# Hashed attention and a SwiGLU block: who adds up the sums for the last block, and when two rows are rounded

## The chip, the core and the metric

The kernel runs on one core of a Trainium2 chip, as one program. The metric is the device time of an execution in microseconds. Five engines work side by side, each through its own instructions: TensorE (PE in the profile; its weight loads are PEld), VectorE (DVE), ScalarE (ACT), GpSimd (POOL) and SyncE (SP), which here only issues DMAs. Transfers are issued from SP, ACT and POOL.

## The reference

Attention in which a query sees only keys of its own hash bucket, and then a gated feed-forward block on its output, cut to what matters:

```python
# q, k, v: (4, 8, 768, 64) float32; proj: (64, 6)
q_bucket = sum over bits of (q @ proj > 0) * 2**bit        # k_bucket likewise
scores = where(q_bucket == k_bucket, q @ k.T / 8, -1e9)
attn = exp(scores - max) / sum
x = (attn @ v), heads side by side                         # (3072, 512)
g, val = x @ w_gate, x @ w_val                             # (512, 1536), float64
out = (g * sigmoid(g) * val) @ w_out                       # w_out (1536, 512), float64
```

The change touches only the second half, the feed-forward block.

## The kernel before, in words

**Blocks.** The 3072 tokens are worked on in three blocks of 1024 (`NB` = 3). Attention ends at about 314 us of the profiled execution. In the first two blocks there are twelve rows of the hidden layer, f = 0 to 11, of 128 features each. A row has an *up product* U f: four pieces (`atoms_of`), the first products `a` of gate and of value, then the second products `n` of gate and of value. Every operand is split into a rounded high part, a low part and their scaled difference, so that TensorE's products keep the precision: `a` is the product of high and low, `n` the correction. ScalarE copies `a` into the bank of `n` (L852), the second product is added onto it, ScalarE makes the gate from it (L865), VectorE the product of gate and value (L876). The result is rounded into `hid` in a *tail*: high part on ScalarE (L885), low part and difference on VectorE (L896, L899). A tail runs a given number of pieces later, counted in `tails`.

**Down products.** After three rows each stands a *down product* D n: eight chunks of 128 tokens. From the second part on, a chunk's accumulator is first copied into PSUM (`sow`, L927); after the product ScalarE copies the sum back (L972) and VectorE subtracts the correction (L978). So the order in the second block is U0 to U3, D0, U4 to U6, D1, U7 to U9, D2, U10, U11, D3. PSUM is four pairs of banks taken in turn: chunk 4 of a down product takes the pair of chunk 0 and can begin when chunk 0's L972 and L978 are done.

**The third block** computes its up products with fewer multiplications: over pairs of rows, in the manner of Strassen and Winograd, with seven products in place of eight. It needs sums of weight pieces and four sums of x. These are made *during the second block*, in tiles `made` (tag x2 for gate and for the first of x's sums, x3 for value and for the second), rounded there as well, and stored in DRAM (`sums_ram`, `xsums`) until the third block loads them. For each of six pairs of rows (p = 0 to 5) and for gate and value: `keep_w` adds the parts of the even row (VectorE, L1089), `add` the odd row and then the four combinations (L1102 to L1111), then come `high` (ScalarE, L1131), `low` and `diff` (VectorE, L1137 and L1156 for weights, L1139 and L1159 for x). `low` and `diff` each issue a store from SP. A tile x2 or x3 can be written again only when its stores have landed.

**Which engine adds.** In `add` before, gate's weight sums run on VectorE, value's on GpSimd for p = 0 to 4 and on VectorE for p = 5 (which is made at the end of the first block). All of x's sums, xa, xb, ya, yb, run on GpSimd (L1119 to L1125): two subtractions for the first of a pair, four for the second.

**The order around the change** is written by hand. `at_` and the loop over xa, xb, ya, yb name, for each sum, after which piece its steps are recorded: "U 5 3" is after piece 3 of row 5, "D 1 4" after chunk 4 of down product 1. What is recorded earlier stands earlier on its engine. The loads of weights from DRAM into the six ring buffers (`bring`, L308) are issued from POOL, in the same order as its sums; the stores and the loads of x are issued from SP.

Of the kernel before, what the change touches and what calls it, by code (L numbers as in the profile page):

```python
# [13 lines left out]
ALU = mybir.AluOpType  # L14
# [5 lines left out]
def kernel(  # L20
# [31 lines left out]
    nc = tc.nc  # L52
    PSUM = bass.MemoryType.PSUM
    B, H, S, D = q.shape
# [6 lines left out]
    NP = H // 2  # L61
# [3 lines left out]
    NF = DF // P  # L65
    PIECE = 512
# [70 lines left out]
    n = 0  # L137
# [654 lines left out]
    def gated_block(scope):  # L792
# [11 lines left out]
        LAST = NB - 1  # L804
# [248 lines left out]
        tails = []  # L1053
# [10 lines left out]
        def split_x(block, pr):  # L1064
            return split(raw_x.pop((block, pr)), block, pr, 0, WB)

        raw_x = {}
# [6 lines left out]
        made = {}  # L1074
        kept_w = {}
        tt = nc.vector.tensor_tensor
        k0, k1 = slice(0, HP), slice(HP, PIECE)

        def make(key, load=True):

            kind, n, side = key
            t = made[key] = xparts_p.tile([P, 2, 3, PIECE], FP32, tag=f"x{2 + side}", name="made")
            if load:
                for e in range(2):
                    nc.sync.dma_start(t[:, e, 0::2], ram[place["gv"[side], 2 * n + e]].bitcast(FP32)[:, 0:2])
# [3 lines left out]
            tt(w, held[what, F][:, 0].bitcast(FP32), held[what, F][:, 1].bitcast(FP32), op=ALU.add)  # L1089

        def add(key, F=None):

            kind, n, side = key
            tt = (nc.vector if kind == "w" and (F is None or side == 0) else nc.gpsimd).tensor_tensor
            if kind == "w":
                if F is not None:
                    make(key, False)
                t = made[key]
                if F is not None:
                    piece = held["gv"[side], F].bitcast(FP32)  # L1100
                    a, c = kept_w.pop("gv"[side]), t[:, 1, 2]
                    tt(c, piece[:, 0], piece[:, 1], op=ALU.add)  # L1102
                else:
                    a, c = t[:, 0, 2], t[:, 1, 2]
                    tt(a, t[:, 0, 0], a, op=ALU.add)
                    tt(c, t[:, 1, 0], c, op=ALU.add)
                s1, s2, s3, s4 = t[:, 0, 1, k0], t[:, 0, 1, k1], t[:, 1, 1, k0], t[:, 1, 1, k1]
                tt(s1, c[:, k0], c[:, k1], op=ALU.add)
                tt(s3, a[:, k0], c[:, k0], op=ALU.subtract)
                tt(s2, s1, a[:, k0], op=ALU.subtract)  # L1110
                tt(s4, a[:, k1], s2, op=ALU.subtract)  # L1111
                return
            make(key, False)
            t = made[key]
            b11, b12, b21, b22 = (raw_x[LAST, n + e][:, half * PIECE : (half + 1) * PIECE]
                                  for e in (0, NP // 2) for half in range(2))
            one, two_ = t[:, 0, 1], t[:, 1, 1]
            if side == 0:
                tt(one, b12, b11, op=ALU.subtract)  # L1119
                tt(two_, b22, one, op=ALU.subtract)  # L1120
            else:
                tt(one, b22, b12, op=ALU.subtract)
                tt(two_, b12, b11, op=ALU.subtract)
                tt(two_, b22, two_, op=ALU.subtract)
                tt(two_, b21, two_, op=ALU.subtract)  # L1125
                for e in (0, NP // 2):
                    raw_x.pop((LAST, n + e))

        def high(key):
            t = made[key]  # L1130
            nc.scalar.activation(r32(t[:, :, 0]), t[:, :, 1], AF.Copy,  # L1131
                                 scale=TOWARD if key[0] == "w" else TOWARD / STEP)
# [30 lines left out]
        def add_late(key, F):  # L1163
            add(key, F)
            bring()
# [8 lines left out]
        def put(kind, f, at, op, *args):  # L1174
            plan.setdefault((kind, f, at), []).append(lambda: op(*args))
# [7 lines left out]
        put("U", 0, 3, low, first_v)  # L1183
        put("U", 0, 3, diff, first_v)
        at_ = {
            0: ("U 1 1", "U 1 3", "U 2 1", "U 2 2", "U 2 3", "U 2 3", "U 3 0", "U 3 0"),
            1: ("U 3 1", "U 3 3", "D 0 2", "D 0 3", "D 0 4", "D 0 4", "D 0 5", "D 0 6"),
            2: ("U 5 3", "U 6 0", "U 6 1", "U 6 2", "U 6 3", "D 1 0", "D 1 1", "D 1 2"),
            3: ("U 7 3", "U 8 0", "U 8 1", "U 8 2", "U 8 3", "U 8 3", "U 9 0", "U 9 1"),
            4: ("U 9 3", "D 2 0", "D 2 2", "D 2 3", "D 2 4", "D 2 5", "D 2 6", "D 2 7"),  # L1190
        }

        def spot(text):
            kind, f, at = text.split()
            return kind, int(f), int(at)

        for p in range(NG - 1):
            g, v = ("w", p, 0), ("w", p, 1)
            F = (LAST - 1) * NF + 2 * p
# [12 lines left out]

        put("U", 4, 1, bring, NQ - 1)
        xa, xb, ya, yb = (("x", j, side) for j in range(2) for side in range(2))
        for key, here in ((xa, ("D 0 6", "U 4 2", "U 4 3", "U 4 3")), (xb, ("U 4 0", "U 5 0", "U 5 1", "U 5 1")),
                          (ya, ("D 1 3", "D 1 6", "D 1 7", "U 7 0")), (yb, ("D 1 4", "U 7 1", "U 7 2", "U 7 2"))):
            for text, op in zip(here, (add, high, low, diff)):
                put(*spot(text), op, key)

        xs = {}  # L1220
# [44 lines left out]
        for i, (kind, n) in enumerate(order):  # L1265
            b, f = divmod(n, NF if kind == "U" else NF // NQ)
            if b == LAST - 1:
                if kind == "U" and f == NF - 2:
                    assert not made
                    steps = first_quarter()  # L1270
                    put("U", f, 2, steps[0])
                    put("U", f, 3, steps[1])
                    put("U", f + 1, 0, steps[2])
                    put("U", f + 1, 0, load_x, LAST, (NP - 1,))
                    put("U", f + 1, 1, bring_sum, 0, xparts_p, "x3")
            elif (kind, f) == ("D", NF // NQ - 2):
                load_x(b + 1, range(NP // 2))
            elif kind == "U" and f >= NF - 2:
                assert len(added) == NPIECE
                splits.extend(split_x(b + 1, f - NF + 2))  # L1280
                if f == NF - 1:
                    load_x(b + 1, range(NP // 2, NP))
            for at, atom in enumerate(gens.pop(i, None) or atoms_of(kind, n)):
                if kind == "U" and at == 2:
                    sow_next(i)
                tail = atom()
                for entry in list(tails):
                    entry[0] -= 1
                    if not entry[0]:
                        tails.remove(entry)  # L1290
                        entry[1]()
                if tail:
                    tails.append([1 if n % NF == NF - 1 else 2, tail])
                if kind == "U" and f >= NF - 2 and at and splits:
                    splits.pop(0)()
                if kind == "D" and f == NF // NQ - 1:
                    if at == 0:
                        more = [split_x(b + 1, pr) for pr in range(NP // 2, NP)]
                        if b == LAST - 1:
                            for i_ in (1, 2):  # L1300
                                bring_sum(i_, xparts_p, f"x{i_ - 1}")
                    if b == LAST - 1:
                        if at in (1, 2, 5, 7, 8, 9):
                            more[at in (2, 7, 9)].pop(0)()
                        if at in (0, 5, 7):
                            fourth_sum()
                    elif at in (0, 7, 10):
                        for x in more:
                            x.pop(0)()
                count[0] += 1  # L1310
                if left and count[0] in (4, 6, 11):
                    left.append(left.pop(0)())
                    left[:] = [f for f in left if f]
                    if count[0] == 4:
                        bring(2)
                if kind == "U":
                    pace = (1, 2, 2, 2)
                elif n == 0:
                    pace = (0, 0, 0, 2, 1, 2, 2, 2)
                else:  # L1320
                    pace = (0, 0, 1, 0) + (1,) * 8
                if b == LAST - 1:
                    for op in plan.pop((kind, f, at), ()):
                        op()
                    continue
                if b == LAST - 2 and (kind, f) == ("D", NF // NQ - 1):
                    for op, key in opening.get(at, ()):
                        op(key)
                for _ in range(pace[at]):
                    step = next(mine, None)  # L1330
                    if step:
                        step()
# [173 lines left out]
    with ExitStack() as scope:  # L1506
        gated_block(scope)
# [32 lines left out]
```

## Time and profile before

| what | value |
|---|---|
| three runs | 903.12, 909.99 and 901.87 us, median 903.12 |
| profiled execution | 907.07 us, of which the span from first to last instruction is 905.2 |
| mean granted TensorE clock | 0.998 |
| second block in the profile | 511 to 721 us |
| second block (515 to 717 us), busy us | PE 192.13, PEld 155.58, DVE 137.05, ACT 93.98, POOL 68.84 |
| the same, DMA engines | 0.83 busy, 309 GB/s |
| L1102 to L1111 on VectorE | 5 instructions, 0.68 us for 512 columns, 0.42 for 256 |
| L1102 to L1111 on GpSimd | 1.3 to 2.4 us for 512 columns, 0.74 to 1.8 for 256 |
| L1119 to L1125 on GpSimd | 1.3 to 2.2 us each |
| ring load, from issue to landing | 6.9 us (median), 768 KB |

How to read the lines: L852 is line 852 of the kernel; `n<-a` is what is written and what is read, by the program's names; `x8` is how many instructions stand in one line of a timeline; the bracket gives the idle time of that engine before it and what ended it. Times are microseconds from the start of the span.

### The profile page before, as it was taken

Reading aid. Unit: us, or ns where it says so; the run is one execution under the profiler, and the core shown is the slowest. Engines: PE = TensorE matmul, PEld = TensorE weight load, DVE = VectorE, ACT = ScalarE, POOL = GpSimd, SP = SyncE. Lnnn points to the kernel's source line nnn. Section 1 sums busy time; section 2 is a strip of 40 time slices with the busy share of each in tenths; the row PEclk is TensorE's granted clock in tenths of the full one; section 3 lists DMA queues with packets and bytes.
Section 4 is the critical chain, followed back from the end, with each engine's and each line's share of the span. In section 5 each row is a group of like instructions: output and inputs, shape, how many; then the busy total and the mean of one; then the engine's idle time right before and its main releaser. Section 6 shows DMA issues by size and latency. Waiting matters only on the chain.

```text
span 905.2 us, 12871 instructions
## 1 busy us (share of the span) xinstructions
PE 891.1 (98%) x4731; PEld 624.6 (69%) x4731; DVE 671.2 (74%) x840; ACT 532.0 (59%) x782; POOL 158.5 (18%) x248
## 2 busy tenths in 40 slices
PE   9999999999999999999999999988999999999998
PEld 5444444444444488888888788866878788888887
DVE  6779999989999956649484968658673768377387
ACT  6788988788888645541424244344363677276460
POOL 2001100010101210101010021525342122121120
PEclk9999999999999999999999999999999999999999
DMA  7657788878988699776757777686879998397382
GB/s 181 110 146 181 188 209 189 204 184 249 223 190 228 220 356 351 268 266 215 277 193 275 290 305 279 239 330 244 325 289 388 381 341 332 113 339 274 147 289 93
DMA packets 155934, 224.08 MB, mean 248 GB/s; under 512 B 104320, under 2 KB 114016, under 8 KB 155488
## 3 DMA queue, kind: packets, MB, share of 16 engines
q0 software_dynamic: 25312, 128.99, 40.4%
q1 hardware_dynamic: 128576, 90.98, 34.5%
q10 hardware_dynamic: 1984, 3.29, 1.1%
q8 instruction: 37, 0.61, 0.3%
q14 instruction: 25, 0.20, 0.1%
HBM read 157.81 MB, written 64.59 MB: 246 GB/s over the span
## 4 chain that ended last, share of the span: by engine, by line
PE 87%; DVE 4%; DMA 3%; issue 3%; POOL 2%; ACT 1%; SPq 0%; POOLq 0%; DVEq 0%; ACTq 0%
PE o L809 19%; PE sc L605 17%; PE a L809 16%; PE av L636 14%; PE n L809 8%; PE y L809 6%; DMA xsums<-made 2%; PE x L809 2%; PE joint L677 1%; PE z L809 1%; PE joint L497 1%; DMA ring<-ram 1%; DVE o L978 1%; DVE o L974 1%; PE idle L431 0%
## 5 line engine op out<-in xcount | busy, mean ns | idle before, releaser
L809 PE MATMUL o<-ring,hid 128*128 128x512 f32 (+1 forms) x872 | 200.9, 389 | 4.0 <-ACT o L927 3.6
L809 PEld LDWEIGHTS o<-ring,hid 128*128 128x128 f32 x872 | 162.1, 188 | 41.2 <-ACT o L927 5.2
L809 PE MATMUL a<-xparts,ring 128*128 128x512 f32 x768 | 179.6, 392 | 2.6 <-DMA ring<-ram 2.6
L809 PEld LDWEIGHTS a<-xparts,ring 128*128 128x128 f32 x768 | 145.0, 189 | 33.9 <-issue 3.6
L615 ACT ACTIVATE A<-sc 128x768 f32<-128x768 f32 x192 | 154.0, 815 | 1.6 <-PE sc L605 0.8
L605 PE MATMUL sc<-qT,kT 64*128 64x384 f32 x768 | 153.0, 483 | 0.0
L852 ACT ACTIVATE n<-a 128x1024 f32<-128x1024 f32 x46 | 46.3, 1008 | 142.8 <-PE a L809 139.4
L636 PE MATMUL av<-A,vraw 128*64 128x386 f32 (+1 forms) x768 | 127.7, 488 | 0.0
L308 POOL DMA_DIRECT2D ring<-ram x108 | 61.1, 567 | 299.7 <-PE n L809 105.4
L636 PEld LDWEIGHTS av<-A,vraw 128*64 128x64 f32 x768 | 53.7, 136 | 73.3 <-issue 62.4
L605 PEld LDWEIGHTS sc<-qT,kT 64*128 64x128 f32 x768 | 68.8, 187 | 39.9 <-issue 35.3
L809 PE MATMUL n<-xparts,ring 128*128 128x512 f32 x384 | 91.7, 390 | 3.6 <-ACT n L852 3.6
L978 DVE TENSOR_TENSOR o<-o 128x512 f32<-128x512 f32 x84 | 56.9, 685 | 43.4 <-ACT o L972 28.0
L809 PEld LDWEIGHTS n<-xparts,ring 128*128 128x128 f32 x384 | 71.8, 188 | 19.7 <-ACT n L852 4.9
L896 DVE SCALAR_TENSOR_TENSOR hid<-hid,v 128x1024 fp32r<-128x1024 f32 (+1 forms) x26 | 29.8, 1145 | 69.4 <-ACT hid L885 69.4
L605 PE MATMUL sc<-qb,kb 64*128 64x384 bf16 x384 | 63.5, 323 | 0.0
L972 ACT ACTIVATE o<-o 128x512 f32<-128x512 f32 x56 | 33.0, 596 | 46.1 <-PE o L809 45.4
L659 DVE SCALAR_TENSOR_TENSOR both<-A 128x1536 f32<-128x1536 f32 x32 | 55.5, 1733 | 3.9 <-ACT A L615 2.5
L663 DVE TENSOR_TENSOR both<-both,A 128x1536 f32<-128x1536 f32 x32 | 55.9, 1748 | 1.7
L809 PE MATMUL y<-xparts,ring 128*128 128x512 f32 x216 | 54.8, 389 | 0.0
L203 POOL DMA_DIRECT2D ram<-stage x22 | 12.0, 546 | 204.8 <-DVE stage L201 96.1
L809 PEld LDWEIGHTS y<-xparts,ring 128*128 128x128 f32 x216 | 40.5, 188 | 8.4
(224 smaller groups left out, 1123.0 us busy)
## 6 DMA issues: line engine op xcount, KB each, us to landing
ring<-ram POOLq DMA_DIRECT2D x96, 768.0 KB, 6.9
ring<-sums_ram POOLq DMA_DIRECT2D x24, 768.0 KB, 6.6
ram<-stage POOLq DMA_DIRECT2D x22, 768.0 KB, 5.3
sums_ram<-made SPq DMA_DIRECT2D x12, 1024.0 KB
ram<-stage SPq DMA_DIRECT2D x14, 768.0 KB
vraw<-in_v_dram SPq DMA_DIRECT2D x16, 384.0 KB
words<-xram SPq DMA_DIRECT2D x12, 512.0 KB
sums_ram<-made SPq DMA_DIRECT2D x12, 512.0 KB
```

The source lines that it names most:

```text
L203: queues[0].dma_start(ram[i].bitcast(FP32), st)
L308: nc.gpsimd.dma_start(t.bitcast(FP32)[:, :, cols], src[:, :, cols])
L605: nc.tensor.matmul(banks_of[u][:, h], x["k", n][rows, ks], x["q", n][rows, qs], start=start, stop=stop)
L615: nc.scalar.activation(weights(u)[:, :, 0:HQ], banks_of.pop(u), AF.Exp, scale=SCALE * (1.0 if units[u][0] else OFF / 2))
L636: nc.tensor.matmul(ps[h * D : (h + 1) * D, 0:width], raws["v", n][:, h, c, :], a[:, h, 0:width], start=c == 0, stop=c == NCH - 1)
L659: nc.vector.scalar_tensor_tensor(out=t, in0=first, scalar=S * EPS / P / 2, in1=now, op0=ALU.add, op1=ALU.add)
L663: nc.vector.tensor_tensor(t, t, now, op=ALU.add)
L809: nc.tensor.matmul(ps, w, x, start=start, stop=stop, **more)
L852: nc.scalar.activation(n_, a, AF.Copy, scale=-(STEP + 1))
L896: nc.vector.scalar_tensor_tensor(out=l_, in0=h_.bitcast(FP32), scalar=-STEP, in1=v_, op0=ALU.mult, op1=ALU.add)
L972: nc.scalar.activation(accs[c], t[:, 0], AF.Copy, scale=STEP + 1)
L978: nc.vector.tensor_tensor(accs[c], accs[c], t[:, 1], op=ALU.subtract)
```

## The change

In the second block all weight sums are made on VectorE. Of x's sums GpSimd makes the first subtraction of each of the four (`open_x`), VectorE the others, some pieces later. Steps are recorded at other pieces: value's `add` of p = 2, 3 and 4 one or two pieces later, value's roundings of p = 0 to 4 mostly one or two pieces earlier, some of x's roundings in the same pieces as before and its openings where the whole sum began. The tails of rows 6 and 9, which were recorded two pieces after their row, are recorded four and eight pieces after it, which is inside D1 and at the end of D2. Nothing else is changed; TensorE's instructions are the same, in the same order.

```diff
         def add(key, F=None):
             kind, n, side = key
-            tt = (nc.vector if kind == "w" and (F is None or side == 0) else nc.gpsimd).tensor_tensor
             if kind == "w":
...
-            make(key, False)
             t = made[key]
...
             if side == 0:
-                tt(one, b12, b11, op=ALU.subtract)
                 tt(two_, b22, one, op=ALU.subtract)
             else:
-                tt(one, b22, b12, op=ALU.subtract)
                 tt(two_, b12, b11, op=ALU.subtract)
                 tt(two_, b22, two_, op=ALU.subtract)
                 tt(two_, b21, two_, op=ALU.subtract)
...
+        def open_x(key):
+            kind, n, side = key
+            make(key, False)
+            near, far = ((raw_x[LAST, n + e][:, half * PIECE : (half + 1) * PIECE])
+                         for e, half in (((NP // 2, 1), (0, 1)) if side else ((0, 1), (0, 0))))
+            nc.gpsimd.tensor_tensor(made[key][:, 0, 1], near, far, op=ALU.subtract)
...
         at_ = {
-            0: ("U 1 1", "U 1 3", "U 2 1", "U 2 2", "U 2 3", "U 2 3", "U 3 0", "U 3 0"),
-            1: ("U 3 1", "U 3 3", "D 0 2", "D 0 3", "D 0 4", "D 0 4", "D 0 5", "D 0 6"),
-            2: ("U 5 3", "U 6 0", "U 6 1", "U 6 2", "U 6 3", "D 1 0", "D 1 1", "D 1 2"),
-            3: ("U 7 3", "U 8 0", "U 8 1", "U 8 2", "U 8 3", "U 8 3", "U 9 0", "U 9 1"),
-            4: ("U 9 3", "D 2 0", "D 2 2", "D 2 3", "D 2 4", "D 2 5", "D 2 6", "D 2 7"),
+            0: ("U 1 1", "U 1 3", "U 2 1", "U 2 2", "U 2 3", "U 2 2", "U 3 0", "U 3 0"),
+            1: ("U 3 1", "U 3 3", "D 0 2", "D 0 3", "D 0 4", "D 0 3", "D 0 5", "D 0 6"),
+            2: ("U 5 3", "U 6 1", "U 6 1", "U 6 2", "U 6 3", "U 6 3", "D 1 0", "D 1 1"),
+            3: ("U 7 3", "U 8 2", "U 8 1", "U 8 2", "U 8 3", "U 8 3", "U 9 0", "U 9 1"),
+            4: ("U 9 3", "D 2 1", "D 2 2", "D 2 3", "D 2 4", "D 2 4", "D 2 5", "D 2 6"),
         }
...
-        for key, here in ((xa, ("D 0 6", "U 4 2", "U 4 3", "U 4 3")), (xb, ("U 4 0", "U 5 0", "U 5 1", "U 5 1")),
-                          (ya, ("D 1 3", "D 1 6", "D 1 7", "U 7 0")), (yb, ("D 1 4", "U 7 1", "U 7 2", "U 7 2"))):
-            for text, op in zip(here, (add, high, low, diff)):
+        for key, here in ((xa, ("D 0 6", "U 4 1", "U 4 2", "U 4 3", "U 4 3")),
+                          (xb, ("U 4 0", "U 4 3", "U 5 0", "U 5 1", "U 5 1")),
+                          (ya, ("D 1 3", "D 1 5", "D 1 6", "D 1 7", "U 7 0")),
+                          (yb, ("D 1 4", "D 1 7", "U 7 1", "U 7 2", "U 7 2"))):
+            for text, op in zip(here, (open_x, add, high, low, diff)):
                 put(*spot(text), op, key)
...
                 if tail:
-                    tails.append([1 if n % NF == NF - 1 else 2, tail])
+                    wait = 1 if n % NF == NF - 1 else 2
+                    if b == LAST - 1:
+                        wait = {6: 4, 9: 8}.get(n % NF, wait)
+                    tails.append([wait, tail])
```

The entries of a row in `at_` are, in order: `add` of gate, `add` of value, `high`, `low`, `diff` of gate, `high`, `low`, `diff` of value.

## The prediction

> **What bounds the kernel now.** I read the page's busy times, then PE's waits, then the timelines of the second block (511 to 721 us) engine by engine. The busy times:
>
> ```profile
> PE 891.1 (98%) x4731; PEld 624.6 (69%) x4731; DVE 671.2 (74%) x840; ACT 532.0 (59%) x782; POOL 158.5 (18%) x248
> ```
>
> The waits of PE (who waited for whom: us in total, times, longest):
>
> ```profile
> PE n L809 <- ACT n L852: 3.6, 3, 1.9
> PE o L809 <- ACT o L927: 3.6, 2, 2.1
> PE a L809 <- DMA ring<-ram: 2.6, 1, 2.6
> ```
>
> TensorE bounds it. Apart from 1.0 us at the start and 0.2 near the end, all its waits lie in the second block, where the change is. PE's timeline there (start, length, in brackets the wait before it):
>
> ```profile
> 593.00 2.11 PE L809 MATMUL n<-xparts,ring 128*128 128x512 f32 x8 [1.55 <-ACT n L852]
> 597.72 8.92 PE L809 MATMUL a<-xparts,ring 128*128 128x512 f32 x32 [2.61 <-DMA ring<-ram]
> ...
> 618.99 6.46 PE L809 MATMUL o<-ring,hid 128*128 128x512 f32 x27 [2.12 <-ACT o L927]
> 626.92 4.40 PE L809 MATMUL o<-ring,hid 128*128 128x512 f32 x18 [1.48 <-ACT o L927]
> ...
> 662.24 3.93 PE L809 MATMUL n<-xparts,ring 128*128 128x512 f32 x16 [1.91 <-ACT n L852]
> ```
>
> In the chain a clean up product takes 7.25 (a) + 3.63 (n) = 10.88 us, a clean down product 16.32. The block has twelve and four: 12 x 10.88 + 4 x 16.32 = 195.8. It took 721.12 - 510.99 = 210.1. So **14.3 us are lost there**: the five waits above and one of 0.17 make 9.8; the matmuls after the 597 gap run 1.5 slow (clock 0.88 in 597.72 to 610.14); the last down product 0.7 slow; the rest is slow matmuls in the second down product (D1). More than 14.3 can't be won.
>
> Who causes the waits, in the timelines of POOL and ACT:
>
> ```profile
> 583.50 1.28 POOL L1122 TENSOR_TENSOR made<-words 128x512 f32<-128x512 f32 x1 [7.70 <-DMA sums_ram<-made]
> ...
> 590.89 2.13 POOL L308 DMA_DIRECT2D ring<-ram  x4
> ...
> 609.85 1.28 POOL L1102 TENSOR_TENSOR made<-ring 128x512 f32<-128x512 f32 x1 [8.22 <-DMA xsums<-made]
> ```
>
> ```profile
> 590.98 1.06 ACT L1131 ACTIVATE made<-made 128x1024 fp32r<-128x1024 f32 x1 [3.87 <-POOL made L1125]
> ...
> 660.21 1.06 ACT L1131 ACTIVATE made<-made 128x1024 fp32r<-128x1024 f32 x1 [6.90 <-POOL made L1111]
> ```
>
> A sum on GpSimd first waits until the tile's previous contents have landed in DRAM, then takes 4 to 8 us. ScalarE's rounding (L1131) waits for it, and behind that stand the copies that TensorE needs (L852, L927). The ring loads queue behind the sums on POOL as well: those of 590.89 were late for 597.72. Only the wait at 626.92 is VectorE's own.
>
> **What the Trainium skill says.** "Perfetto Trace Analysis", Tensor Engine Instruction: ScalarE, VectorE and GpSimd run strictly in order. The trace agrees: L852 at 591.94 waits behind L1131 though its input was ready. "GPSIMD Engine Reference", Specifications: GpSimd shares its SBUF interface with VectorE when VectorE has two SBUF inputs. It agrees: L1137 takes 1.22 us alone and 2.31 at 623.32, beside POOL's L1120. "DMA: Bandwidth & Descriptors", Anatomy: a DMA costs about 2 us fixed, mostly the write receipt, plus bytes over 436 GB/s; and under Issuing engines: queues of different engines interleave on the same 16 engines. Here stores of `made` landed 4 to 11 us after their last pass, in traffic of some 390 GB/s.
>
> **The change, part by part.**
>
> (1) Weight sums of v: 25 instructions leave POOL for DVE. One set on DVE is 2.19 us (534.24 to 536.43), so 5 x 2.19 = 11.0 more on DVE. Of x's twelve subtractions eight go to DVE at 0.68 (L1105's row) = 5.4; four stay on POOL at 1.3. Against this, DVE loses its slowing beside POOL: in the block L1137 12 x 0.22, L1156 12 x 0.08, L1159 and L1139 4 x 0.8 together, two L899 at +1.0, one kept_w at +1.0 make about 9.7. DVE's busy time, 137 us of 515 to 717, becomes 144: under 75%, so on the mean it isn't the bound.
>
> (2) No sum on POOL now holds the ring loads beyond the wait of x's opening, and ScalarE waits for VectorE instead. But **the wait for the store moves too**: the v sum now stands on DVE, and DVE's in-order queue holds whatever comes after. I walk the new order with the durations above, place by place.
>
> First v sum (U1): the store lands at 538.64, the sum ends 540.8, DVE's next hid needs ACT at 542.7: free.
>
> Second v sum (U3, before D0). DVE reaches it after L876 at 559.4; the store it waits for is issued as before, and landed then at 563.15 (POOL's timeline):
>
> ```profile
> 563.15 1.38 POOL L1102 TENSOR_TENSOR made<-ring 128x512 f32<-128x512 f32 x1 [5.41 <-DMA sums_ram<-made]
> ```
>
> DVE's timeline of the kernel before at this place, where the sum will stand between the two lines:
>
> ```profile
> 558.19 1.22 DVE L876 SCALAR_TENSOR_TENSOR v<-n,g 128x1024 f32<-128x1024 f32 x1
> 559.32 1.30 DVE L978 TENSOR_TENSOR o<-o 128x512 f32<-128x512 f32 x2
> ```
>
> Behind it stand the L978 of D0's chunks 0 and 1, which free the PSUM banks of chunks 4 and 5. Sum ends 563.15 + 2.19 = 565.3, L978 at 566.0; chunk 4 wants to start at 555.02 + 4 x 2.04 = 563.2. **New stall 2.8 us.** The later chunks then meet theirs. U4 starts 574.1 (was 571.34).
>
> x's first pair (U4, U5): POOL opens xa at about 578 and xb at about 584, when the stores have landed. DVE ends xb's sum at 591.3, ScalarE rounds until 592.4, L852 ends 593.4; second matmuls of v start 594.1. Free, so the 1.55 is gone. Ring loads for U6 go out right after xb's opening, at about 585 instead of 590.89; at the table's 6.9 us to landing they are there by 592, needed at 595.9. The 2.61 goes, and with it the slow clock (1.5).
>
> D1: U6 ends 606.8. DVE rounds U5's hid from 605.2, reaches the third v sum at 607.6. xb's stores leave DVE at 599.3; before they took 11 us with four ring loads in front, which now ran earlier, so I take 6 to 8: no wait. Sum ends 609.8, ScalarE's rounding 610.9, L972 and L927 for chunk 2 by 611.9; its second half wants 612.2. L876 ends 612.1, chunk 3 wants 612.9. L978 of chunk 0 ends 614.5, chunk 4 wants 615.0. Everything fits by 0.3 to 0.9 us, because U6's hid rounding (2.4 us) moves behind four chunks (`wait` 4). Cost taken: 0.3. With 11 us it would be 2.6.
>
> U8, U9: the fourth v sum is reached at 646.1, stores of y land about 642 to 646; L852 of U9 needs ScalarE at 648.8 and has 2 us to spare: the 1.91 goes. D2: the fifth waits for stores ending about 658 + 6 = 664 and frees chunk 6 by 667.2 (needed 668.4); U9's hid rounding moved behind the chunks lets it. SP: same stores and x loads, but one x load goes behind the fifth v store's first part; it is needed only in D3 (before: loaded at 679.5, read at 707.8). x's later slots add nothing else.
>
> Sum: left are 2.8 (D0) + 0.3 (D1) + 0.2 + 0.7 (last down product) = 4.0, and 1.2 for the thin margins (3 in 10 for D1's 2.6 and D2's 0.8 if landings are long, and some slow clock after stalls). 14.3 - 5.2 = **9.1 us won**. The profiled execution, 907.07 (905.2 and 1.9 around it), becomes 898.0. It is 4.0 above the median of 903.12, inside the runs' spread; from the median: **894.0**. Unknown ends: landing times, from D0's stall 0 to D1's 2.6 and more.
>
> **The rivals.**
>
> Half kept: stores land as late as before, so DVE stalls D0 2.8, D1 2.6, D2 0.8, slow clock 1.5, and 0.9 as above: 8.6 lost, 5.7 won, 897.4. For it: 8.22 and 9.02 us of waiting in front of POOL's sums. Against: those stores shared the DMA engines with four ring loads.
>
> All hidden: the store before D0 lands 3 us earlier. Loss 1.2, won 13.1, 890.0. For it: a ring load that POOL held back until 542.90 goes out at about 539.4. Against: the store is issued after 551.7 and finds the same traffic.
>
> Slower: VectorE takes over GpSimd's waits in full. If the third and fourth v sums wait 8.2 and 9.0 us from the points of the walk, TensorE stalls 7.9 in D1 and 9.0 + 2.2 + 1.0 + 1.9 less slack, 6.8, in U9; with D0 2.8, D2 2.0, slow clock 3.0 and 0.9: 23.4 lost, 9.1 more than now, 912.2. It decides from where those two landings pass about 12 to 14 us after DVE's last pass. Against: 10.5 and 11.2 before, with more traffic.
>
> **How the numbers follow.** Forecast 0.48 (own range 890.5 to 898), half kept 0.22, all hidden 0.18, slower 0.12. The range of 889.0 to 901.0 takes in the first three with a margin. About 1% is what a measurement of this kernel can tell from no change: 894.1 and 912.2. Half of the forecast, all hidden and a little of the second lie below 894.1: faster 0.45; slower 0.10; the rest 0.45.
>
> **What would show it.** Right: the waits of L852 on TensorE and of L308's four loads are gone; a new gap of 2 to 3 us in the middle of D0 with DVE's v sum waiting for the store before it; the weights' low pass (L1137 before) at 1.22 us throughout; TensorE's idle time in the block under 5 us. Wrong: gaps in D1 or U9 ended by ScalarE or VectorE after a v sum's wait; ring loads still late at U6; no gap in D0 (store earlier than taken).

## The result and the profile after

| kernel | median, us | runs |
|---|---|---|
| before | 904.93 | 901.87 to 909.99 |
| changed | 895.55 | 894.87 to 895.79 |

The ratio is 0.9887, interval [0.9853, 0.9922]: about 9.4 us, or 1.1%, faster; 894.0 was predicted. The profiled execution took 894.87 us (span 892.8) where the one of before took 907.07, so between the two profiles it is 12.2 us. The runs also lie closer together: 0.9 us from lowest to highest, against 8.

Busy times, from the page of the changed kernel. POOL has lost 46 us, DVE gained 5.4:

```profile
PE 887.1 (99%) x4731; PEld 622.9 (70%) x4731; DVE 676.6 (76%) x873; ACT 532.1 (60%) x782; POOL 112.4 (13%) x215
```

PE's waits inside the second block of the changed kernel (total, times, longest). The n and a rows shown of before are gone, and of the o row one wait is left:

```profile
PE o L809 <- ACT o L927: 1.0, 1, 1.0
```

PE's timeline of the changed kernel at D0, U6 and D1:

```profile
554.52 16.48 PE L809 MATMUL o<-ring,hid 128*128 128x512 f32 x72
...
592.61 7.42 PE L809 MATMUL a<-xparts,ring 128*128 128x512 f32 x32
...
603.52 4.37 PE L809 MATMUL o<-ring,hid 128*128 128x512 f32 x18
608.87 12.54 PE L809 MATMUL o<-ring,hid 128*128 128x512 f32 x54 [0.97 <-ACT o L927]
```

The first line is all of D0, 72 matmuls without a gap. The second is U6, 7.42 us instead of 8.92 and without the 2.61 ahead of it. The only gap is in D1. The block now runs from 510.58 to 708.99, 198.4 us. Against 195.8 in the chain 2.6 are lost, where before lost 14.3.

DVE's timeline of the changed kernel around D0, which the prediction walked through with a landing at 563.15:

```profile
557.70 1.22 DVE L876 SCALAR_TENSOR_TENSOR v<-n,g 128x1024 f32<-128x1024 f32 x1
559.34 0.69 DVE L1100 TENSOR_TENSOR made<-ring 128x512 f32<-128x512 f32 x1 [0.43 <-DMA sums_ram<-made]
...
561.54 1.28 DVE L978 TENSOR_TENSOR o<-o 128x512 f32<-128x512 f32 x2
```

The second v sum stands where the prediction put it, and does wait for the store, but for 0.43 us: the store landed at 559.34. L978 follows at 561.54, early enough for chunk 4. What had changed ahead of it is in POOL's timelines, first of the kernel before, then of the changed one:

```profile
542.90 1.10 POOL L308 DMA_DIRECT2D ring<-ram  x2
```

```profile
539.25 0.53 POOL L308 DMA_DIRECT2D ring<-ram  x1 [3.77 <-DVE made L1106]
542.29 0.53 POOL L308 DMA_DIRECT2D ring<-ram  x1 [2.51 <-PE n L809]
```

Of the two ring loads that went out together at 542.90 before, behind the first v sum, one now goes at 539.25.

The groups of VectorE (total, mean ns | idle before) show the weights' low pass, before at 1442 ns in the mean and now at its undisturbed time:

```profile
L1137 DVE TENSOR_TENSOR made<-made 128x1024 fp32r<-128x1024 f32 x12 | 17.3, 1442 | 0.4 <-ACT made L1131 0.4
```

```profile
L1140 DVE TENSOR_TENSOR made<-made 128x1024 fp32r<-128x1024 f32 x12 | 14.6, 1217 | 0.0
```

### The profile page after: what moved, and what is told of

The parts are those of the page before. It is cut to its first block, busy times and chain, and to the rows that moved or that the text cites. A ratio compares the mean times of both kernels' runs of the same rounds, so it can differ in the third digit from the quotient of the medians.

```text
span 892.8 us, 12863 instructions
## 1 busy us (share of the span) xinstructions
PE 887.1 (99%) x4731; PEld 622.9 (70%) x4731; DVE 676.6 (76%) x873; ACT 532.1 (60%) x782; POOL 112.4 (13%) x215
## 4 chain that ended last, share of the span: by engine, by line
PE 92%; DVE 3%; issue 2%; DMA 1%; POOL 0%; ACT 0%; SPq 0%; POOLq 0%; DVEq 0%; ACTq 0%
PE o L809 20%; PE a L809 19%; PE sc L605 18%; PE av L636 14%; PE n L809 9%; PE y L809 6%; PE x L809 2%; PE joint L677 1%; PE z L809 1%; PE joint L497 1%; DMA ring<-ram 1%; DVE o L974 1%; DVE o L978 1%; DMA landing<-in_q_dram 0%; POOL ring L308 0%
## 5 line engine op out<-in xcount | busy, mean ns | idle before, releaser
L978 DVE TENSOR_TENSOR o<-o 128x512 f32<-128x512 f32 x84 | 56.8, 684 | 36.2 <-ACT o L972 20.7
L605 PEld LDWEIGHTS <-kb 64*128 64x128 bf16 x384 | 19.6, 94 | 32.5 <-issue 9.0
```

What stands on the lines that cost most here:

```text
L605: nc.tensor.matmul(banks_of[u][:, h], x["k", n][rows, ks], x["q", n][rows, qs], start=start, stop=stop)
L978: nc.vector.tensor_tensor(accs[c], accs[c], t[:, 1], op=ALU.subtract)
```

## The experiments

The theory: three parts. (A) The gain is the second block's waits on GpSimd's sums. (B) The predicted stall in D0 is real for a late landing, and is absent because ring loads that are no longer held back let the store land earlier. (C) The gap in D1 comes from ScalarE's third v rounding, which stands ahead of the L927 that a chunk's first matmul waits for. Rivals: the gain is x's lighter load or the later tails; it is VectorE running without GpSimd beside it, so that it grows with the share of work moved; the landing doesn't depend on the ring loads.

### One part at a time

**v's sums alone (e1).** The kernel before with its weight sums on VectorE and the new places of v's steps; x's sums and the tails as before. Against the changed kernel, x's sums go back to GpSimd and to their old places (shown in part):

```diff
+            gp = nc.gpsimd.tensor_tensor
+            make(key, False)
...
-                tt(two_, b22, one, op=ALU.subtract)
+                gp(one, b12, b11, op=ALU.subtract)
+                gp(two_, b22, one, op=ALU.subtract)
```

> The weight sums of value on VectorE at their new pieces, x's sums wholly on GpSimd as before, tails of rows 6 and 9 as before. Theory (each sum taken off GpSimd's queue removes the waits behind that sum, and no others): the stalls of U9 (1.91) and of D1 behind the v sum (2.12) are gone, those behind xb's sum stay (1.55 in U5, 2.61 and the slow clock 1.5 in U6), D1 has 1 to 2 us because row 6's tail stands in front of its chunks. Loss in the block 7 to 9 us against 14.3 before and 2.6 after: 899 to 902 in a profiled execution. Rival (most of the gain is VectorE running without GpSimd beside it, so it grows with the share of work moved): v's 25 of 33 instructions bring three quarters of it, about 897.5, with no stall in U6.

Measured: 898.33 us, ratio 0.9924 [0.9901, 0.9947]. That is below the theory's 899 to 902 and near the rival's 897.5. The theory's reason doesn't fit either: the gaps in U5 and U6 were gone though x's sums still stood on GpSimd (e8 shows why). A new one came, the only long one in the block (PE's timeline of this kernel):

```profile
606.89 15.71 PE L809 MATMUL o<-ring,hid 128*128 128x512 f32 x68 [2.42 <-DMA ring<-ram]
```

This ring load was issued late, at 599.90, after gate's sum had waited 1.74 us for xa's stores.

**x's split alone (e2).** The other half: `open_x` and the new places of x; v's sums on GpSimd at their old places, tails as before.

> Only x's sums are split between GpSimd and VectorE; value's weight sums stay on GpSimd at their old pieces, tails as before. Theory: U5 and U6 run without a gap (5.7 us won with the clock), D1's wait behind the v sum of the third pair and U9's behind the fourth stay, 2 to 4 us each. About 899 to 901. Rival (share of moved work): 8 of 33 instructions, about a quarter of the gain, 903.

Measured: 903.32 us, 0.9981 [0.9964, 0.9998], 1.4 us below the median of before on that chip. This too is the rival's number (903) and not the theory's. PE's waits in the block of this kernel:

```profile
PE o L809 <- DMA ring<-ram: 3.2, 3, 2.0
PE o L809 <- ACT o L927: 2.1, 2, 1.6
```

The gaps in U5, U6 and U9 were absent, but the down products waited for ring loads and for L927 instead. So x's part alone moves most of its loss to the next place.

Both times are what the share of moved work gives. The rival's reason is not what the traces show: in D2 the late ring loads (0.83 and 1.96 us) went out from 650.52 on, behind the fourth v sum on POOL, and the longest wait for L927 (1.64) comes from a rounding that waited for the third v sum. Only one of 0.43 was VectorE's, as in the kernel before only the 1.48. What VectorE's slowing beside GpSimd costs was not measured apart, since no run took it away alone.

**The tails as before (e3)**, everything else changed.

```diff
-                    if b == LAST - 1:
-                        wait = {6: 4, 9: 8}.get(n % NF, wait)
```

> The changed kernel with the tails of rows 6 and 9 two pieces after their row, as before. Theory: VectorE's 2.4 us of hid rounding stand in front of chunk 2's subtraction in D1 and D2; chunks 6 wait 1 to 2 us in D1 and 0.5 in D2: 897 to 898. Rival (the later tails are not needed once the sums have moved): no new stall, 895.5.

Measured: 897.56 us, 0.9916 [0.989, 0.9941]: 2.0 us above the changed kernel. As the theory said, chunk 6 of D1 now waits, beside the gap that the changed kernel has (PE's timeline of this kernel):

```profile
618.85 4.37 PE L809 MATMUL o<-ring,hid 128*128 128x512 f32 x18 [1.62 <-ACT o L927]
```

**The tails alone (e8)**, in the kernel before.

> The kernel before with the two later tails alone (row 6's rounding behind four pieces, row 9's behind eight). Theory: the tails stand in VectorE's queue ahead of L978, so they cost only where VectorE is the last to come, which in the kernel before is the gap of 1.48 us at 626.92 in D1 and, behind it, a little in D2; the waits caused by GpSimd's sums (1.55 in U5, 2.61 in U6, 2.12 in D1, 1.91 in U9) stay. Expected: 1 to 2 us faster than before, ratio about 0.998 to 0.999, with those four gaps still there. Rival: the 2 us that the tails are worth in the changed kernel come only from there, because its VectorE does the weight sums; then the kernel before gains nothing (within 0.5 us) and keeps a gap of over 1 us at about 627.

Measured: 904.23 us, ratio 1.0008 [0.9987, 1.0029]. The theory missed: no gain can be seen, and the interval leaves room for 1.2 us at most. So the 2.0 us of the later tails show only where VectorE makes the v sums. The rival has the time right, but not the trace: the gap at 626.92 is gone. PE's timeline of this kernel shows what took its place:

```profile
604.00 1.21 PE L809 MATMUL o<-ring,hid 128*128 128x512 f32 x4 [0.60 <-ACT o L927]
606.12 5.50 PE L809 MATMUL o<-ring,hid 128*128 128x512 f32 x23 [0.90 <-DMA ring<-ram]
613.24 10.50 PE L809 MATMUL o<-ring,hid 128*128 128x512 f32 x45 [1.62 <-ACT o L927]
655.59 5.54 PE L809 MATMUL n<-xparts,ring 128*128 128x512 f32 x16 [2.84 <-ACT n L852]
```

There is something else in it. Up to D1 every engine runs the kernel before, instruction by instruction, and yet it has no gap in U5 or U6. The stores (SP's timeline, of the kernel before and of this one) and POOL's timeline of this kernel tell why:

```profile
546.46 5.77 SPq L1148 DMA_DIRECT2D sums_ram<-made  x4
```

```profile
545.65 5.77 SPq L1148 DMA_DIRECT2D sums_ram<-made  x4
```

```profile
559.44 1.29 POOL L1102 TENSOR_TENSOR made<-ring 128x512 f32<-128x512 f32 x1 [2.45 <-DMA sums_ram<-made]
...
579.69 1.28 POOL L1122 TENSOR_TENSOR made<-words 128x512 f32<-128x512 f32 x1 [1.70 <-DMA sums_ram<-made]
```

In this execution the store ahead of the second v sum landed at 559.44, not at 563.15, and xb's sum started at 579.69 instead of 583.50. This trace runs 0.8 us ahead here: counted from the first of the four stores, the landing took 13.8 us against 16.7. So the 4.2 us of gaps in U5 and U6 of before, and the slow clock after them, belong to an execution with a late landing. Not every execution has one. It fits that e1, where the store landed early, lacked those gaps. Late landings may be a part of the spread of 8 us, but with one traced execution of the kernel before that isn't shown.

### When the store lands

**The first v sum back on GpSimd (e4)**, everything else changed.

```diff
...
+            eng = nc.gpsimd if kind == "w" and F is not None and side == 1 and n == 0 else nc.vector
...
-                    tt(c, piece[:, 0], piece[:, 1], op=ALU.add)
+                    eng.tensor_tensor(c, piece[:, 0], piece[:, 1], op=ALU.add)
...
```

> The changed kernel with one sum put back: value's weight sum of the first pair (p = 0, in U1) on GpSimd. It tests why D0 had no stall. Theory (the two ring loads that this sum holds back until 542.9 push the stores of that pair back; in the changed kernel they go out at 539.25 and 542.29): the stores land at about 563 instead of 559, VectorE waits 3 to 4 us before the second v sum, chunk 4 of D0 waits 2 to 3 us: 898. Rival (the landing at 559 has another cause, or is chance from run to run): no wait over 1 us before the second v sum, no gap in D0, 895.5.

Measured: 898.32 us, 0.9926 [0.9902, 0.9951]. In this kernel's trace, POOL's ring loads, DVE's second v sum, and PE in D0:

```profile
543.07 1.10 POOL L308 DMA_DIRECT2D ring<-ram  x2
```

```profile
562.65 0.69 DVE L1101 TENSOR_TENSOR made<-ring 128x512 f32<-128x512 f32 x1 [3.15 <-DMA sums_ram<-made]
```

```profile
565.58 10.07 PE L809 MATMUL o<-ring,hid 128*128 128x512 f32 x36 [2.15 <-DVE o L978]
```

This is the stall that was predicted (2.8 us in the middle of D0), by the same chain: ring loads held until 543, landing at 562.65, sum, L978, chunk 4. It cost more than the gap: the 36 matmuls behind it took 9.91 us where 8.16 is clean, at a granted clock of 0.83.

All profiles together: where the first v sum is on GpSimd and holds the loads (before, e2, e4, e8), the second v sum's wait for the store ended at 563.15, 561.23, 562.65 and 559.44, which is 16.7, 15.1, 16.0 and 13.8 us after the first of the four stores was issued. Where it is on VectorE, no wait for it lasted past 559.8, or 13.5 us after that issue, in any of nine profiles. So the landing depends on the held loads, and they make a late one possible; they don't force it. The times of this kernel fit: three of its eleven executions took 895.6 to 896.6, close to the changed kernel, the others 897.8 to 900.3. What decides between 13.8 and 16.7 us in one and the same program isn't settled, nor what happens in the DMA queues between load and store.

**The first two v sums alone on VectorE (e7)**, in the kernel before.

```diff
-            tt = (nc.vector if kind == "w" and (F is None or side == 0) else nc.gpsimd).tensor_tensor
+            tt = (nc.vector if kind == "w" and (F is None or side == 0 or n < 2) else nc.gpsimd).tensor_tensor
```

> The kernel before with only two edits of the change: value's weight sums of the first two pairs (p = 0 and 1) on VectorE, all else as before, x's sums on GpSimd. Theory (the late second v sum is the root of the chain: its stores land late, xb's sum starts late, and ScalarE's rounding and U6's ring loads are late behind it): no gap in U5 and U6 although x's sums weren't touched, D1's waits and U9's 1.91 stay; 5 to 6 us won, about 899. Rival (xb's own length on GpSimd causes those gaps): they stay, under 1.5 us won, 903 to 904.5.

Measured: 902.38 us, 0.9969 [0.9954, 0.9985], 2.8 to 3.1 us won instead of 5 to 6. PE's waits in the block of this kernel:

```profile
PE o L809 <- ACT o L927: 2.5, 2, 1.5
PE n L809 <- ACT n L852: 2.2, 2, 2.0
PE o L809 <- DMA ring<-ram: 1.1, 1, 1.1
```

The gaps in U5 and U6 are absent, which after e8 proves less than it was meant to. What the theory had not: D1 kept a late ring load (1.09 us) and two waits for L927 (0.98 and 1.50), and U9 a wait of 2.0. The third and fourth v sums are still on GpSimd there.

### What is left in D1

**v's third rounding one piece later (e5)**, behind D1's chunk instead of ahead of it.

```diff
-            2: ("U 5 3", "U 6 1", "U 6 1", "U 6 2", "U 6 3", "U 6 3", "D 1 0", "D 1 1"),
+            2: ("U 5 3", "U 6 1", "U 6 1", "U 6 2", "U 6 3", "D 1 0", "D 1 0", "D 1 1"),
```

> The changed kernel with value's rounding of the third pair recorded after chunk 0 of D1 in place of after U6, so that on ScalarE the copies of chunks 0 and 2 stand ahead of it. Theory (a chunk's first matmul already waits for its L927, so the 0.97 us gap in D1 is L927 of chunk 2 standing behind the rounding that waits for VectorE's sum): the gap goes, 894.5. Rival (only the second half of a chunk waits for L927, and the gap is VectorE being full): L978 and L876 decide, gap stays or moves to chunk 4, 895.5.

ScalarE's timelines, first of the changed kernel, then of this one:

```profile
606.78 1.06 ACT L1134 ACTIVATE made<-made 128x1024 fp32r<-128x1024 f32 x1 [1.85 <-DVE made L1109]
607.74 0.58 ACT L972 ACTIVATE o<-o 128x512 f32<-128x512 f32 x1
608.22 0.59 ACT L927 ACTIVATE o<-o 128x512 f32<-128x512 f32 x1
```

```profile
606.53 0.60 ACT L972 ACTIVATE o<-o 128x512 f32<-128x512 f32 x1 [1.02 <-PE o L809]
607.02 0.59 ACT L927 ACTIVATE o<-o 128x512 f32<-128x512 f32 x1
607.54 1.05 ACT L1134 ACTIVATE made<-made 128x1024 fp32r<-128x1024 f32 x1
```

L927 ends 1.2 us earlier by the traces' clocks, 1.8 counted from the start of D1 (603.52 and 604.10), because L1134 now stands behind it. Of the gap in D1 0.3 us are left at most (in the second trace of this kernel), ended by a ring load. The time: 894.76 us (0.9893 [0.9862, 0.9925]) against the changed kernel again on that chip:

> The changed kernel once more, to stand beside the next kernel on the same chip. Both theories: 895.5, all runs within 1 us of each other.

Measured: 895.4. As 0.6 us is little, both were measured once more, side by side.

> The same kernel as e5_rounding_after_chunk, beside the changed kernel on one chip. Theory: the 1.0 us gap of D1 is gone, so it is 0.6 to 1.0 us faster than the changed kernel (ratio 0.999). Rival: the time moves to the next limit and the two agree within 0.3 us.

> The changed kernel again, on the chip of e9_rounding_after_chunk_again, for comparison: 895 to 896 us, gap of about 1.0 us in D1.

Measured: 894.91 (893.98 to 895.74) against 895.46 (895.36 to 895.9). Taking all runs together, 7 of this kernel's 11 lie below every one of the changed kernel's 17. So it is the fastest version here, by about 0.6 us, a little under what the gap was worth.

**GpSimd kept busy during D1 (e6).** 24 additions of 128 columns on GpSimd, of a tile that nothing reads, four at each of D1's first six chunks. They are added work and change no output.

> The changed kernel with 24 additions on GpSimd in D1 that nothing reads (128 columns each, about 0.5 us, in an SBUF tile of their own), four after each of chunks 0 to 5. It measures what GpSimd beside VectorE costs by itself, with no sum in anybody's way. Theory A (sharing SBUF slows VectorE's passes with two SBUF inputs, 1.22 to about 2 us): VectorE has some 4 us more in D1, chunks 4 to 6 wait, 3 to 5 us lost, 899 to 900. Theory B (the slowing is small against the waits): under 1 us, 895.5 to 896.5.

Measured: 902.23 us, 0.9961 [0.9944, 0.9977], 6.7 us more than the changed kernel, and by neither expectation's way. VectorE's two-input passes of 1024 columns were slowed from 1.22 to 1.42 us at most. The trace of this kernel (its lines stand 3 further down) shows the group of additions, then POOL's loads, then PE at U7:

```profile
L1230 POOL TENSOR_TENSOR beside<-beside 128x128 f32<-128x128 f32 x24 | 17.7, 736 | 1.7
```

```profile
633.28 1.62 POOL L308 DMA_DIRECT2D ring<-ram  x3
```

```profile
640.04 6.58 PE L812 MATMUL a<-xparts,ring 128*128 128x512 f32 x16 [4.34 <-DMA ring<-ram]
```

One addition takes 0.74 us, and 17.7 us of them stand in POOL's queue ahead of three ring loads, which go out at 633.28 instead of 623.17. PE then waits 4.34 us, and the 16 matmuls behind the wait take 6.42 us instead of 3.63, at a granted clock of 0.55. Together that is 7.1 of the 7.8 us between the two spans (900.6 and 892.8). So this work cost through the ring loads behind it, and hardly through VectorE's speed.

## Why the prediction was right, and where it wasn't

**Time and direction.** 894.0 predicted, 895.55 measured, inside the range; a gain of 9.1 against 9.4. That these lie so close is in part luck, since two errors of opposite sign meet. The profiled gain was 12.2 (11.7 of it in the second block) where 9.1 was worked out, because the stall in D0 and most of the margin were not paid. And the profiled execution of before, with its late landing, lost more than most: 69 of 103 executions of that kernel took less than its 907.07. The prediction carried its gain over to the median unchanged.

**"New stall 2.8 us" in D0: failed.** The failed term is the landing time. The prediction took 563.15 from the kernel before, because the store "finds the same traffic". It landed at 559.34; counted from the issue of the stores (545.87 against 546.46) that is 3.2 us sooner. This is the mechanism of the rival "all hidden", down to its ring load at about 539.4, and no gap in D0 was among the prediction's own signs of being wrong. The rest of the step was right: with a late landing (e4) the stall comes at its place, 2.15 us, and 1.75 of slow matmuls behind it.

**"Its second half wants 612.2", cost 0.3 in D1: mis-sized.** Already the first matmul of a chunk waits for its L927. The kernel before shows it: its wait of 2.12 for L927 comes after 27 matmuls, which are three whole chunks of nine. In the changed kernel PE was free for chunk 2 at 607.9 and L927 ended at 608.8: 0.97 us, and D1 as a whole took 1.4 more than a clean down product. e5 took the rounding away from ahead of L927 and the gap went.

**U5, U6, U9 and the slow clock: gone, as said.** But the 1.55 in U5, the 2.61 in U6 and the 1.5 of slow clock were counted as if every execution paid them. e8 shows an execution that doesn't. The term was read rightly from one profile and is probably too large for the median. One reading in the sum of 14.3 is wrong: of the 2.2 us of slow matmuls that it puts into D1, 1.1 are there, the others in U0, U5 and U9. The sum stays.

**Later tails that let D1 fit: right.** With the tails as before, D1 waits 1.62 us more and the kernel takes 2.0 more (e3). The prediction named this; it did not say that the tails alone, in the kernel before, bring nothing that can be seen (e8).

**VectorE doesn't become the bound: right.** The low pass is at 1.217 us; DVE's busy time in 515 to 707 is 144.4 us, predicted 144. The rival "slower" needed landings some 12 us after DVE's last pass; the longest wait of a sum for a store on DVE was 1.76 us:

```profile
636.09 0.69 DVE L1100 TENSOR_TENSOR made<-ring 128x512 f32<-128x512 f32 x1 [1.76 <-DMA xsums<-made]
```

**Where the gain came from, by parts** (differences of medians): v's sums alone 6.4 us, x's split alone 1.4, the tails alone nothing; together 9.4. That v's sums are most of it is shown. That the parts help each other is seen in the tails (e3 against e8) and in the waits that each part alone leaves behind; in the sum of the times it isn't clear of the noise.

## What to carry to other kernels

When work moves from a queue that also issues DMAs, follow the DMAs first: they go out earlier, and a store that competes with them can land earlier too, so a landing time must not be carried over from the old trace unchanged. Before a gap is counted as a gain, ask whether it hangs on a landing: then one profile shows one draw, and a second execution of the same program can be without it. Look for copies that TensorE waits for (here L927) right behind a conversion on an in-order engine; moving one behind them cost nothing here.

## What the runs showed of the hardware

- In two executions of what is, up to there, the same program, a store landed 13.8 and 16.7 us after the first of its group of four was issued (545.65 to 559.44 in e8, 546.46 to 563.15 in the kernel before).
- TensorE can run slow behind a wait, and the length of the wait doesn't say how much. Behind 2.15 us (e4) the matmuls up to the end of D0 took 1.75 us more than clean ones, at a granted clock of 0.83, and behind 4.34 us (e6) the next 16 took 2.8 more, at 0.55. Behind 2.42 us (e1) the rest of D1 ran within 0.2 us of clean, at 1.00.
- A GpSimd addition of 128 columns took 0.74 us, as long as the shortest with 256 columns (0.74 to 1.8). Beside such small ones VectorE's two-input pass of 1024 columns took 1.23 to 1.42 us, beside GpSimd's 256-column sums 1.65 (e8 at 561.85), and beside its 512-column sums (before, and e7 at 617.06) 2.31, against 1.22 alone. "GPSIMD Engine Reference", Specifications, in the Trainium skill says that the two share an interface, with contention when VectorE has two SBUF inputs. The runs agree, and show that the price depends on what GpSimd does; which property of its operands decides was not separated.
